# First output units of an attention and spectral-mixing kernel: another order of products, copies and PSUM banks

## The chip, the cores and the metric

The kernel runs on one core of a Trainium2 chip. The metric is the device time of one execution in microseconds (us). Before the change three runs gave 438.65, 438.73 and 439.03 us, median 438.73 us. Engines are called as in the profile: PE (TensorE, matmuls), DVE (VectorE), ACT (ScalarE), POOL (GpSimd), SP (SyncE). POOL and SP also issue DMAs; SP issues all DMAs that write the output.

## The reference

Sliding-window attention with a linear distance bias is followed by a mixing of the 64 lowest Fourier modes along the sequence, and by a channel product with ReLU. Batch 8, 8 heads of 64 channels, so 512 channels; 576 positions; float32 in and out.

```
scores = where(0 <= i-j < 128, q k^T / sqrt(D) - slope_h |i-j|, -1e9)
x      = softmax(scores) v                     # [8, 576, 512], heads side by side
X      = rfft(x, axis=positions)
Y[:64] = X[:64] (w_r + i w_i)                  # one 512x512 pair of matrices per mode
u      = x + irfft(Y)
out    = u + relu(u @ w_ch)
```

The weights w_r and w_i are 64 matrices of 512x512 each, 134 MB in all; the output is 9.44 MB.

## The kernel before, in words

**Two long stages and a tail.** The attention runs while the first weights load. Then the products of the modes with their weights (L886) follow the weight DMAs, sixteen groups of four modes ("quads"). What the tail needs is prepared beside them: `project` leaves `XW` = x @ w_ch and `augment` changes `x` in place, both with the lower 32 modes already in. The upper 32 modes come late. Their spectra stand as rows of `Z` (per batch pair), and `ZW` holds Z @ w_ch. The last quad, modes 60 to 63, depends on the last weight matrix; its rows are `yq`, and `yw` is yq @ w_ch.

**The tail: 18 output units.** A unit is two batches by 128 positions by 512 channels, 512 KB of output. Units 8 and 17 hold the last 64 positions of four batches each. Units 0 to 3 need batches 0 and 1, units 4 to 7 batches 2 and 3, unit 8 batches 0 to 3, units 9 to 12 batches 4 and 5, units 13 to 16 batches 6 and 7, unit 17 batches 4 to 7. For each unit:

- `mm` in PSUM is XW, brought in by products with an identity (`begin`, `restore`, L762; L758 for units 8 and 17), plus the late modes from `ZW` (`channels`, L659; L772). `activate` then makes `r` = relu(mm) on ACT (L802).
- `yy` in PSUM is x plus the late modes from `Z` (`add_tokens`, `finish_tokens`, the same lines).
- `finish` adds `o` = yy + r on DVE (L842) and SP writes `o` to the output (L844; L851 for units 8 and 17). `o` has 5 buffers.

`mm` and `yy` are each one tile of two PSUM banks (`pair`), one bank per batch, n = 0 and 1. There are two slots of four banks. Slot 0 is opened within the last quad, slot 1 after the last quad's own products.

**Modes 60 to 63.** Units 0 and 1 get them by one product per half with `FM` (`last_rows`, L786) from `yq` and `yw`. All others read them from `Z` and `ZW`, into which `patch` copies them by small DMAs on SP or POOL (L648), one per batch: 6 KB or 2 KB or 8 KB.

**Unit 0 is done in halves and by other engines.** `with_tokens` adds the last modes to yy of half n and ACT copies it into `o` (L816); `finish_first` adds the last modes to mm of half n, DVE computes o = max(mm, 0) + o (L823), and SP writes that half (L825). Units named in `HALVES` run ACT, DVE and the output DMA once per half instead of once per unit.

**What sets the order.** All engines run their instructions in program order, written out by hand. Before, the order behind the last weight product is: transposes of the last quad (L962); Z patches of batches 0 to 6; yy of unit 0 half 0; yw (L601, L603); mm of unit 1; ZW patches (batches 0 and 1 by SP, 2 to 7 by POOL), Z patch of batch 7; `finish_first`, which between its halves does half 1 of `with_tokens`; then `activate(1)`, `finish(1)`, `activate(2)`, and for j = 3 to 17 `activate(j)`, `finish(j-1)`; at the end `finish(17)`. So mm of unit j stands ahead of yy of unit j-1 on PE. A PSUM slot of mm is free again when ACT has read it, one of yy when DVE has read it.

## Time and profile before

| what | value |
|---|---|
| median of 3 runs | 438.73 us |
| the profiled execution's own time | 437.99 us |
| its span in the profile | 436.1 us |
| busy: PE, DVE, ACT, POOL | 316.2, 184.5, 162.3, 90.2 us |
| last weight product starts (L886) | 402.42 us |
| first output DMA issued (L825) | 406.89 us |
| last output sum on DVE (L842) | 429.48 to 430.16 us |
| output: 23 DMAs, 10 of 256 KB and 13 of 512 KB | 9.44 MB |
| median from issue to landing, 256 KB and 512 KB | 3.4 and 5.0 us |

Positions in time are counted from the start of the span. The profiled execution took 1.9 us more than its span and 0.7 us less than the median of the runs. Durations of single instructions come from this one execution. An idle time that the profile puts down to an engine whose work was long done was a wait for something else that it stood together with, often a DMA.

### The profile page before, as it was taken

How to read it: one execution, taken by the hardware profiler on the slowest of the kernel's cores; microseconds unless marked ns; L12 is line 12 of the kernel's file. 1: busy time of each engine (PE TensorE's matmuls, PEld its weight loads, DVE VectorE, ACT ScalarE, POOL GpSimd, SP SyncE). 2: the span in 40 equal slices, each digit the busy share in tenths (PEclk: the TensorE clock that was granted, in tenths of full speed). 3: DMA queues.
4: the chain of work that ended last, by engine and by line, in shares of the span. 5: the costliest groups of instructions: out<-in, count | busy, mean ns of one | idle time of the engine just before them, and what ended most of it. 6: DMA issues, size and time to landing. Idle time of an engine off the chain costs nothing.

```text
span 436.1 us, 8292 instructions
## 1 busy us (share of the span) xinstructions
PE 316.2 (73%) x3488; PEld 177.7 (41%) x3509; DVE 184.5 (42%) x332; ACT 162.3 (37%) x211; POOL 90.2 (21%) x170
## 2 busy tenths in 40 slices
PE   5589899979686635543442487999889999788982
PEld 4367677757565312111111133444434444334430
DVE  7789799887783301000000021322213233122684
ACT  6949899988681000000000011322222322102780
POOL 8701010103424002222112110101111110012600
PEclk9969999999999955555555569999999999989997
DMA  8999999999999999999999999999999999998598
GB/s 285 326 311 310 290 316 300 307 298 299 252 217 212 215 215 213 214 214 214 215 212 214 214 215 214 215 214 215 215 214 214 215 215 215 213 215 153 190 378 311
DMA packets 50453, 105.54 MB, mean 242 GB/s; under 512 B 4032, under 2 KB 21072, under 8 KB 50416
## 3 DMA queue, kind: packets, MB, share of 16 engines
q0 software_dynamic: 19440, 68.41, 77.9%
q1 hardware_dynamic: 30976, 36.60, 25.3%
q8 instruction: 27, 0.44, 0.4%
q14 instruction: 10, 0.08, 0.1%
HBM read 162.53 MB, written 9.44 MB: 394 GB/s over the span
## 4 chain that ended last, share of the span: by engine, by line
DMA 71%; PE 10%; DVE 8%; issue 5%; POOL 2%; ACT 1%; SPq 1%; DVEq 0%; POOLq 0%; ACTq 0%
DMA w<-in_moe_w_i_dram 42%; DMA wch<-in_moe_w_ch_dram 8%; DMA qr<-in_q_dram 7%; DMA vr<-in_v_dram 6%; DVE o L842 3%; DMA qr<-in_moe_w_i_dram 3%; PE my L702 2%; DMA vr<-in_moe_w_r_dram 2%; DMA kr<-in_k_dram 2%; DVE vb L246 1%; PE acc L886 1%; PE av L344 1%; POOL Z L648 1%; PE my L659 1%; DVE att L318 1%
## 5 line engine op out<-in xcount | busy, mean ns | idle before, releaser
L886 PE MATMUL acc<-w,XC 128*32 128x512 bf16 x456 | 80.3, 478 | 68.5 <-DMA w<-in_moe_w_i_dram 34.2
L886 PEld LDWEIGHTS <-XC 128*32 128x32 bf16 x508 | 38.4, 147 | 109.2 <-issue 82.8
L307 ACT ACTIVATE att<-sc 128x1024 bf16<-128x1024 f32 x64 | 64.1, 1032 | 9.7 <-PE sc L297 9.6
L636 ACT CAST ZW<-zw 128x512 bf16<-128x512 f32 x8 | 4.7, 585 | 142.9 <-PE zw L634 142.9
L344 PE MATMUL av<-vb,att 128*128 128x132 bf16 (+1 forms) x576 | 38.4, 217 | 13.3 <-DVE x L360 8.6
L344 PEld LDWEIGHTS <-att 128*128 128x128 bf16 x704 | 36.6, 98 | 18.7 <-DVE x L360 12.0
L608 DVE TENSOR_SCALAR yq<-acc 128x512 bf16<-128x512 f32 x14 | 9.6, 687 | 81.8 <-PE acc L886 81.8
L702 PE MATMUL my<-wch,xT 128*64 128x512 bf16 x288 | 34.5, 381 | 5.7 <-ACT x L733 4.2
L711 ACT CAST XW<-my 128x512 bf16<-128x512 f32 x36 | 19.3, 589 | 50.5 <-PE my L659 50.5
L683 DVE COPY xT<-tr 128x1024 bf16<-128x1024 bf16 x18 | 12.4, 692 | 54.9 <-PE tr L681 54.9
L269 ACT COPY qkT<-tp 128x1152 bf16<-128x1152 bf16 x30 | 33.5, 1116 | 4.1 <-PE tp L263 3.6
L491 POOL DMA_DIRECT2D w<-in_moe_w_r_dram x22 | 15.6, 710 | 72.1 <-PE acc L886 46.1
L491 POOL DMA_DIRECT2D w<-in_moe_w_i_dram x23 | 16.3, 709 | 64.1 <-PE acc L886 45.3
L297 PE MATMUL sc<-qkT 64*64 64x256 bf16 (+2 forms) x640 | 25.1, 263 | 4.8 <-ACT qkT L269 1.2
L360 DVE TENSOR_TENSOR x<-av,rec 128x640 bf16<-128x640 f32 x32 | 26.4, 825 | 1.1
L702 PEld LDWEIGHTS <-xT 128*64 128x64 bf16 x288 | 17.1, 109 | 21.5 <-issue 9.1
L246 DVE CAST vb<-vr 64x1024 bf16<-64x1024 f32 x32 | 22.6, 708 | 0.2
L733 ACT CAST x<-my 128x512 bf16<-128x512 f32 x18 | 10.5, 585 | 31.6 <-PE my L659 31.6
L297 PEld LDWEIGHTS <-qkT 64*64 64x64 bf16 x640 | 14.5, 109 | 19.1 <-issue 16.0
L734 DVE CAST x<-my 128x512 bf16<-128x512 f32 x18 | 12.4, 692 | 21.7 <-PE my L659 21.7
L842 DVE TENSOR_TENSOR o<-yy,r 128x1024 f32<-128x1024 f32 (+1 forms) x20 | 20.3, 1059 | 2.1 <-ACT r L802 1.9
L318 DVE TENSOR_TENSOR att<-att,mask 128x1024 bf16<-128x1024 bf16 x32 | 20.5, 682 | 0.0
(137 smaller groups left out, 424.7 us busy)
## 6 DMA issues: line engine op xcount, KB each, us to landing
w<-in_moe_w_i_dram POOLq DMA_DIRECT2D x23, 1024.0 KB, 36.2
w<-in_moe_w_r_dram POOLq DMA_DIRECT2D x22, 1024.0 KB, 35.6
qr<-in_q_dram SPq DMA_DIRECT2D x16, 576.0 KB, 7.9
kr<-in_k_dram SPq DMA_DIRECT2D x16, 576.0 KB, 7.9
w<-in_moe_w_r_dram POOLq DMA_DIRECT2D x16, 512.0 KB, 14.2
vr<-in_v_dram SPq DMA_DIRECT2D x56, 128.0 KB, 7.6
w<-in_moe_w_i_dram POOLq DMA_DIRECT2D x13, 512.0 KB, 24.0
out_dram<-o SPq DMA_DIRECT2D x13, 512.0 KB, 5.0
```

The costliest lines, as they stand in the source:

```text
L246: nc.vector.tensor_copy(self.vb[u % 2][row, :, :, :, W * half : W * half + D], src[row, :2])
L269: (self.nc.vector.tensor_copy if u < 2 and w == "q" else self.nc.scalar.copy)(dst.rearrange("q h (p j) -> q h p j", j=TPP), tp.rearrange(" ...
L297: nc.tensor.matmul(sc[64 * half : 64 * half + 64, e, j * 256 + c0 : j * 256 + c0 + n], lhsT=qkT[row, 1, h, k0 + j : k0 + P : 2], rhs=qkT[r ...
L307: self.nc.scalar.activation(self.att[u % 2][:, kt * 8 * P : (kt + 1) * 8 * P], sc.rearrange("p e n -> p (e n)"), AF.Exp, scale=1.0 / math. ...
L318: nc.vector.tensor_tensor(out=rows, in0=rows, in1=self.table[:, heads], op=ALU.mult)
L344: nc.tensor.matmul(bank[:, qt * W : qt * W + rhs[j].shape[1]], lhsT=att[:, o : o + P], rhs=rhs[j], start=(n == 0 and j == 0), stop=(n == l ...
L360: nc.vector.tensor_tensor(out=self.x[:, b, :, cs].rearrange("p t (h d) -> p h t d", h=2), in0=tiles[:, :, :, :D], in1=rec.unsqueeze(-1).br ...
L491: nc.gpsimd.dma_start(out=t.rearrange("p s a e -> p s (a e)"), in_=w[kinds.pop()][m : m + 2].rearrange("m (p a) e -> p m (a e)", a=4))
L702: nc.tensor.matmul(mm[ROWS[half]], lhsT=lhsT, rhs=wch[:, dt], start=(dt == 0), stop=False, skip_group_check=True,)
L711: nc.scalar.copy(XW[:, j, n], mms[n])
L842: nc.vector.tensor_tensor(out=o[:, c], in0=yy[:, c], in1=r[:, c], op=ALU.add)
L886: nc.tensor.matmul(into[32 * (m % 4) : 32 * (m % 4) + 32], lhsT=XC[:, c0 : c0 + 31 * NM + 1 : NM], rhs=wq[t][a], start=(ri == 0 and a == 0 ...
```

## The change

- Each slot is opened by `open_slot` with separate tiles for the two halves ("joint" false: four one-bank tiles mm0, mm1, yy0, yy1), used by unit 0 and unit 1. Later the slot is closed and opened again with pair tiles as before (slot 0 behind `finish_first`, slot 1 behind `finish(1)`).
- Half 1 of unit 0's `with_tokens` moves ahead of unit 1's mm (and out of `finish_first`), and its copy goes to DVE; half 0's stays on ACT.
- Unit 1's `last_rows` and relu alternate by halves.
- `finish` is split: `sums(j)` has yy's products. Order on PE: yy(1), yy(2), mm(2), then for j = 3 to 17 mm(j), yy(j). On DVE and ACT the units' order is as it was.
- Unit 3 joins `HALVES`: two relus, two sums and two output DMAs of 256 KB.
- Patches: SP has only ZW of batch 0. POOL issues Z 1, Z 2, ZW 1, Z 3, ZW 2, ZW 3, then Z 4, Z 5, ZW 4, ZW 5, Z 6, Z 7, ZW 6, ZW 7.

```diff
-        HALVES = (1, 2, len(units) - 1)
+        HALVES = (1, 2, 3, len(units) - 1)
         def pair(tag, slot=0):
-            return heads[tag][slot].tile([P, 2, DM], FP32, tag=tag, name=tag)
+            pool, joint = slots[slot]
+            if joint:
+                t = pool.tile([P, 2, DM], FP32, tag=tag, name=tag)
+                return t, t[:, 0], t[:, 1]
+            return (None, *(pool.tile([P, DM], FP32, tag=tag + str(n), name=tag)
+                            for n in range(2)))
+        def open_slot(slot, joint, **kw):
+            if slot in slots:
+                opened[slot].close()
+            opened[slot] = mctx.enter_context(ExitStack())
+            slots[slot] = opened[slot].enter_context(tc.tile_pool(
+                name=f"s{slot}{joint:d}", bufs=1, space=PSUM, reuse_waits="tile", **kw)), joint
+        def hold(j):
+            slot = idle.pop(0)
+            mms[j] = pair("mm", slot), slot
         def begin(j):
-            slot = idle.pop(0)
-            mm = pair("mm", slot)
-            mms[j] = mm, slot
-            restore(mm, j, XW[:, j])
+            if j not in mms:
+                hold(j)
+            restore(mms[j][0], j, XW[:, j])
         def activate(j):
-            if j == 1:
-                last_rows(mms[j][0], j, heads["yw"])
-            else:
+            if j != 1:
                 begin(j)
                 channels(j)
...
             for c in parts(j):
-                nc.scalar.activation(r[:, c], mm[:, c], AF.Relu)
+                if j == 1:
+                    last_rows(mm, 1, heads["yw"], (c.start,))
+                nc.scalar.activation(whole(r, c), part(mm, c), AF.Relu)
-        def with_tokens(o, n):
+        def with_tokens(o, n, copy):
             last_rows(yys[0][0], 0, heads["yq"], (n,))
-            nc.scalar.copy(o[:, n], yys[0][0][:, n])
+            copy(o[:, n], yys[0][0][1 + n])
         def finish_first(o):
...
                 nc.sync.dma_start(out=out[n, :P], in_=o[:, n])
-                if n == 0:
-                    with_tokens(o, 1)
-        def finish(j):
-            b, st = units[j]
+        def sums(j):
             if j not in yys:
                 take(j)
             add_tokens(j)
             finish_tokens(j)
+        def finish(j):
+            b, st = units[j]
...
-        patch([(nc.gpsimd, b) for b in (2, 3, 4, 5, 6)], yq, lambda b: Z[:, b // 2, 1], 6)
+        patch([(nc.gpsimd, 2)], yq, lambda b: Z[:, b // 2, 1], 6)
...
-        with_tokens(first, 0)
+        with_tokens(first, 0, nc.scalar.copy)
         for i, c in enumerate(sides):
             zl = zps.tile([P, DM], FP32, tag=f"z{i}", name=f"zl{i}")
             late_channels(zl, yT, yw, c)
+        with_tokens(first, 1, nc.vector.tensor_copy)
...
         channel_rows = partial(patch, rows=yw, dst=lambda b: ZW[:, b // 2, 1])
-        channel_rows([(nc.sync, 0), (nc.sync, 1)] + [(nc.gpsimd, b) for b in range(2, B)])
-        patch([(nc.gpsimd, 7)], yq, lambda b: Z[:, b // 2, 1], 6)
+        channel_rows([(nc.sync, 0), (nc.gpsimd, 1)])
+        patch([(nc.gpsimd, 3)], yq, lambda b: Z[:, b // 2, 1], 6)
+        channel_rows([(nc.gpsimd, b) for b in (2, 3)])
+        for b in range(4, B, 2):
+            patch([(nc.gpsimd, b), (nc.gpsimd, b + 1)], yq, lambda b: Z[:, b // 2, 1], 6)
+            channel_rows([(nc.gpsimd, b), (nc.gpsimd, b + 1)])
         finish_first(first)
+        open_slot(0, True)
+        hold(2)
         activate(1)
+        sums(1)
+        sums(2)
         finish(1)
+        open_slot(1, True, side="right")
         activate(2)
+        finish(2)
+        take(3)
+        hold(3)
         for j in range(3, len(units)):
             activate(j)
-            finish(j - 1)
-        finish(len(units) - 1)
+            sums(j)
+            finish(j)
```

More of the change, by code (lines that the diff above doesn't have):

```diff
@@ L581 @@
         ps = pctx.enter_context(tc.tile_pool(name="fps", bufs=1, space=PSUM))
-        heads, free, idle = {}, [], []
+        heads, slots, opened, free, idle = {}, {}, {}, [], []
         def late_end(acc):
@@ L734, in augment, with part, whole @@
             nc.vector.tensor_copy(src[:, 1], ys[1])
-        HALVES = (1, 2, len(units) - 1)
+        HALVES = (1, 2, 3, len(units) - 1)
         mms, yys, rs = {}, {}, {}
         def pair(tag, slot=0):
-            return heads[tag][slot].tile([P, 2, DM], FP32, tag=tag, name=tag)
+            pool, joint = slots[slot]
[10 more added lines that the diff above has]
+                name=f"s{slot}{joint:d}", bufs=1, space=PSUM, reuse_waits="tile", **kw)), joint
+        def part(t, c):
+            return t[0] if c.stop - c.start == 2 else t[1 + c.start]
+        def whole(t, c):
+            return t if c.stop - c.start == 2 else t[:, c.start]
         def take(j):
@@ L757, in restore @@
                 if units[j][1] == FULL:
-                    nc.tensor.matmul(dst[:, n], lhsT=pairs, rhs=src[:, n],
+                    nc.tensor.matmul(dst[1 + n], lhsT=pairs, rhs=src[:, n],
                                      start=True, stop=False, skip_group_check=True)
@@ L762, in restore @@
                     nc.tensor.matmul(
-                        dst[ROWS[row], n], lhsT=ident[ROWS[n], ROWS[n]],
+                        dst[1 + n][ROWS[row]], lhsT=ident[ROWS[n], ROWS[n]],
                         rhs=src[ROWS[n], row], start=True, stop=False, skip_group_check=True,
@@ L771, in late_modes @@
                 if st == FULL:
-                    nc.tensor.matmul(dst[:, n], lhsT=FC, rhs=rows[:, b // 2 + n, 1],
+                    nc.tensor.matmul(dst[1 + n], lhsT=FC, rhs=rows[:, b // 2 + n, 1],
                                      start=False, stop=True, skip_group_check=True)
@@ L775, in late_modes @@
                 for row in range(2):
-                    spread(dst[:, n], row, b + n, 1, st, row, rows)
+                    spread(dst[1 + n], row, b + n, 1, st, row, rows)
         def channels(j):
@@ L785, in last_rows @@
             for n in sides:
-                nc.tensor.matmul(ps[:, n], lhsT=FM[:, n, st * P : (st + 1) * P], rhs=rows,
+                nc.tensor.matmul(ps[1 + n], lhsT=FM[:, n, st * P : (st + 1) * P], rhs=rows,
                                  start=False, stop=True, skip_group_check=True)
@@ L811, in finish_tokens @@
             late_modes(yys[j][0], j, Z)
-        def with_tokens(o, n):
+        def with_tokens(o, n, copy):
             last_rows(yys[0][0], 0, heads["yq"], (n,))
-            nc.scalar.copy(o[:, n], yys[0][0][:, n])
+            copy(o[:, n], yys[0][0][1 + n])
         def finish_first(o):
-            (mm, mm_slot), (_, yy_slot) = mms.pop(0), yys[0]
+            (mm, mm_slot), (_, yy_slot) = mms.pop(0), yys.pop(0)
             for n in range(2):
                 last_rows(mm, 0, heads["yw"], (n,))
-                nc.vector.scalar_tensor_tensor(out=o[:, n], in0=mm[:, n], scalar=0.0,
+                nc.vector.scalar_tensor_tensor(out=o[:, n], in0=mm[1 + n], scalar=0.0,
                                                in1=o[:, n], op0=ALU.max, op1=ALU.add)
                 nc.sync.dma_start(out=out[n, :P], in_=o[:, n])
-                if n == 0:
-                    with_tokens(o, 1)
-            del yys[0]
             idle.append(mm_slot)
             free.append(yy_slot)
-        def finish(j):
-            b, st = units[j]
+        def sums(j):
             if j not in yys:
@@ L841, in finish @@
             for c in parts(j):
-                nc.vector.tensor_tensor(out=o[:, c], in0=yy[:, c], in1=r[:, c], op=ALU.add)
+                nc.vector.tensor_tensor(out=whole(o, c), in0=part(yy, c), in1=whole(r, c),
+                                        op=ALU.add)
                 if st < FULL:
@@ L869 @@
                     pctx.close()
-                    head = mctx.enter_context(
-                        tc.tile_pool(name="hps", bufs=1, space=PSUM, reuse_waits="tile"))
-                    heads.update(mm=[head], yy=[head])
+                    open_slot(0, False)
                     idle.append(0)
@@ L974 @@
             late_channels(zl, yT, yw, c)
+        with_tokens(first, 1, nc.vector.tensor_copy)
         zctx.close()
         lctx.close()
-        last = mctx.enter_context(
-            tc.tile_pool(name="tps", bufs=1, side="right", space=PSUM, reuse_waits="tile"))
-        heads["mm"].append(last)
-        heads["yy"].append(last)
+        open_slot(1, False, side="right")
         idle.append(1)
```

## The prediction

> **What bounds the kernel now.** The page first: its second part shows DMA at 8 or 9 tenths in nearly all slices, with one hole in the third slice from the end. The last weights set when that hole begins (the last L886 product starts at 402.42), and the change touches nothing ahead of it. So I cut the end of the span into windows. Columns: us, busy time of PE, PEld, DVE, ACT, POOL with instruction counts, granted clock, DMA share, GB/s.

> ```profile
> 402.50:407.50 5.00, 3.86 (x31) 1.79 (x35) 1.45 (x4) 2.47 (x7) 3.69 (x8) 1.00 0.05 10
> 407.50:408.80 1.30, 1.17 (x20) 0.53 (x20) 1.00 (x3) 1.30 (x3) 1.30 (x3) 1.00 0.63 214
> 408.80:412.00 3.20, 3.20 (x56) 1.61 (x49) 2.82 (x5) 3.20 (x5) 1.74 (x4) 1.00 0.86 293
> 412.00:416.00 4.00, 3.80 (x48) 1.46 (x45) 3.95 (x5) 3.30 (x4) 0.00 (x0) 1.00 1.00 369
> ...
> 428.00:434.00 6.00, 0.63 (x3) 0.10 (x1) 2.11 (x3) 0.00 (x0) 0.00 (x0) 0.81 1.02 379
> 434.00:436.10 2.10, 0.00 (x0) 0.00 (x0) 0.00 (x0) 0.00 (x0) 0.00 (x0) 0.50 0.06 23
> ```

> The reader is to see three stretches: five us almost without DMA while PE, ACT and DVE make the first results; 4.5 us in which the output flows at 214 and 293 GB/s; and from 412 on a flow of about 379 GB/s to the end. The last sum on DVE ends at 430.16, the flow near 434: behind DVE there are 4 us of queued output. A shorter DVE or ACT step after 413 therefore buys nothing. The time is: start of the output flow, plus 9.44 MB at 379 GB/s (24.9 us), plus what the flow lacks near its start. The lack: from the first bytes at 407.7 to 412.0 the two windows moved 0.28 and 0.94 MB where 4.3 us would carry 1.63, so 0.41 MB or 1.08 us; from 412 to 416 another 0.1. Some 1.2 us are to be had, and more only by starting earlier.

> The chain of waits names DVE L842 for the largest part of the tail; the timeline corrects it. By engine:

> ```profile
> 406.64 0.81 PE L786 MATMUL mm<-F,FM 128*128 128x512 bf16 x3 [0.57 <-DVE o L823]
> ```
> ```profile
> 405.90 0.69 DVE L823 SCALAR_TENSOR_TENSOR o<-mm,o 128x512 f32<-128x512 f32 x1 [1.83 <-DMA Z<-yq]
> 407.13 0.69 DVE L823 SCALAR_TENSOR_TENSOR o<-mm,o 128x512 f32<-128x512 f32 x1 [0.54 <-PE mm L786]
> 408.12 1.29 DVE L842 TENSOR_TENSOR o<-yy,r 128x512 f32<-128x512 f32 x2 [0.30 <-ACT r L802]
> 409.79 7.09 DVE L842 TENSOR_TENSOR o<-yy,r 128x512 f32<-128x512 f32 x7 [0.38 <-ACT r L802]
> ```
> ```profile
> 406.11 0.58 ACT L816 COPY o<-yy 128x512 f32<-128x512 f32 x1 [0.72 <-PE yy L786]
> 407.49 6.90 ACT L802 ACTIVATE r<-mm 128x512 f32<-128x512 f32 x9 [0.79 <-PE mm L786]
> ```
> ```profile
> 405.61 1.22 SPq L648 DMA_DIRECT2D ZW<-F  x2
> 406.89 1.32 SPq L825 DMA_DIRECT2D out_dram<-o  x2
> 408.84 8.44 SPq L844 DMA_DIRECT2D out_dram<-o  x9
> ```

> PE's product for half 1 of unit 0 waited 0.57 us until DVE had read half 0: another bank, but the same tile. Behind it on PE queue the two products of unit 1, so ACT's relu and DVE's sums start late. DVE idles between its first sums (0.54, 0.30, 0.38), and each idle becomes a hole in the output flow. The 1.05 us that DVE idles before 423.84 is put down to ACT's r, which was ready two units earlier; it waits for one of the five o buffers, so for the output DMA.

> **The change part by part.** All starts that follow are estimates from rows of this execution.

> (1) yy half 1 moved ahead of unit 1's mm. The eight L601 products start 0.11 apart from 403.95, so PE is free at 404.82. One 128x512 product costs 0.23 (L786 at 405.47, the next at 405.70) and a change of stationary shape 0.09 (404.91 against 404.82). Unit 1's mm starts 0.23 later, at 405.14, its late modes at 405.38, and unit 0's mm half 0 at about 405.70 instead of 405.47. Cost 0.23 on the path to the first sum: it is done at 406.1 instead of 405.86.

> (2) The copy of half 1 goes from ACT (0.58) to DVE. The row nearest is L823, same source and size: 0.69. It runs from 405.3 to 406.0, under step 1's product, so nothing; without that cover it would cost up to 0.69 ahead of the first output. ACT loses the copy at 406.11.

> (3) First output. The sum runs 406.12 to 406.81 (before 405.90 to 406.59). Before, SP issued it only at 406.89, since its second ZW patch held it until 406.83; that patch goes to POOL. New issue about 406.85. Steps 1 and 3 cancel: the flow starts where it did, give or take 0.2.

> (4) Separate tiles. The wait of 0.57 goes. Half 1's product runs at 405.92, and its sum is next late on DVE alone: back-to-back half sums start 0.61 apart (408.12, 408.73), so 406.73 instead of 407.13. Gain 0.40.

> (5) Unit 1. Its last rows run at 406.14 and 406.36, relu from 406.55 (before 407.49), yy from 406.67 to 407.3. DVE is again what is late: sums at 407.34 and 407.95 instead of 408.12 and 408.73. Gain 0.78.

> (6) Unit 2. yy(2), 0.43 for its eight products, now stands ahead of mm(2); mm(2) must wait for slot 0 in any case, until DVE ends unit 0 at 407.42. mm(2) from 407.5, its ZW products at 407.75, relu at 408.2, sums at 408.8 and 409.4 instead of 409.79 and 410.40. Gain 1.0, if the ZW row of batch 1 is there by 407.75. POOL issues it when unit 1's mm has read ZW, near 405.85, behind Z 1 and Z 2 (done at 404.9), instead of SP at 406.27. From issue to landing, the 8 KB Z patch on POOL took 1.7 in the quiet stretch; POOL's ZW patches took 2.1 to 3.4 within the output flow. The output begins at 407.7, so it is nearest to the 1.7, with 2.1 to 2.4 possible. I take 2.0, landing 407.85: cost 0.1. Ends: 0, and with 3.4 (landing 409.25) 1.5 at this step.

> [...]

> (7) Unit 3 by halves. On DVE 2 x 0.61 for 1.13 (the spacing of full sums, 410.99 to 412.12), on ACT 2 x 0.49 for 0.90; the first half leaves 0.5 us sooner. Sums at 410.0 and 410.6, then unit 4 at 411.2 instead of 412.12: gain 0.9. The two more instructions on DVE and SP lie beside the flow.

> (8) mm(j) then yy(j) instead of a unit's lead. o(j) frees yy of j+2; behind it PE does yy(j+2) and mm(j+3), ACT the relu. Before, with the same pair of products, DVE ended at 422.79 and the relu that followed ended at 424.97: 2.2 us. Two full sums on DVE cover 2 x 1.13, two units of output 2 x 1.38. So nothing; at units 8 and 9, whose products cost 0.43 more, DVE comes late by 0.3 to 0.5, and I find 0.4 us of queued output left there. If that cover were gone it would cost at most 0.1 to 0.3.

> (9) POOL's order. ZW 2 and 3 are issued at about 406.85 and 407.4 as before. Z 4 to ZW 7 end near 412, within the flow instead of before it; with 3.4 to land they are there by 415.5, and unit 9 reads them at 416, units 13 and on after 421. Nothing.

> Sum as output flow: 256 KB take 0.69 us at 379 GB/s. Bytes move 0.85 to 0.9 us after issue (406.89 against 407.7). Issues at 406.85, 407.45, 408.05, 408.65, 409.5, 410.1, 410.75, 411.35 let eight pieces follow one another without a hole from 407.7 to about 413.25; unit 4's issue at 412.45 is due at 413.35. Lack 0.1 there, 0.1 for ZW 1 and about 0.05 for the fact that each single DMA in flight alone ran at 360 rather than 379, instead of 1.2. Gain 0.95: 437.99 becomes 437.04 in terms of the profiled execution. That execution lies 0.74 below the median, so in terms of runs 437.8.

> **The rivals.**

> *The wait stays in another form* (437.4 to 438.3 in runs). If product and sum of unit 0's halves are still held together, or the reopened slot waits for DVE's last read where I let it wait for the copy, PE's rest begins at 406.9: relu(1) at 407.5 as before, but ACT and SP are relieved and yy(2) is ready, unit 4's sum at 411.8 instead of 412.12. Gain 0.35 to 0.6, time 438.25. For it: mm(1) at 404.91 shows waits tile by tile at an earlier reopening, which speaks against; that half 1 waited at all shows that the waits are wider than the data, which speaks for.

> *ZW of batch 1 lands late* (slower). Place: PE at mm(2), with everything behind it. By step 6, landing at X puts unit 4's output issue at X + 4.75 and its bytes at X + 5.65. Before, they were served at 414.5. Break even is X = 408.85, 3.0 us after issue; at the 3.4 of the slowest ZW patch the loss is 0.4 (439.1, within the 0.2%), and from 4.0 it is slower by over 0.2%: 439.7. For it: patches got slower from 2.1 to 3.4 as the output flow set in, and POOL queues a wait for PE ahead. Against: it is issued two us before the first output byte. [...]

> *The lost lead shows* (438.4). If step 8's loop were 3.0 instead of 2.2, DVE would fall to the flow's pace of 1.38 per unit; beyond that the flow would have holes all along. The row is far from it.

> **How the numbers follow.** 0.2% is 0.88 us, about what a measurement of this kernel can tell from no change. Forecast, gain 0.9 to 1.4: chance 0.50. The wait in another form, and the lost lead, together 0.28: within 0.2%. ZW late but under 4 us: 0.12, within 0.2%. ZW later: 0.10, slower. The likeliest time is 437.8, with its own range 437.3 to 437.9; it lies close to the bound, which the sum passes by less than 0.1 us, so faster and same are near each other. Low end 437.2: all of 1.2, and the flow's start 0.3 earlier if SP and step 1 are both kinder. High end 439.2 takes in the late patch at 3.4.

> **What would show it.** Right: no idle on PE before L786 for DVE; DVE without idle from about 405.3 to 411; first output issue at 406.8 to 406.9; unit 4's sum near 411.2; the window from 408.8 to 412 near 370 GB/s; flow over by 433. Wrong: PE idle at mm(2) for a DMA, first output after 407.1, a dip in GB/s near 417 to 420, or DVE idle for ACT in the steady part.

## The result, and the profile after

The changed kernel takes 441.58 us (median of 14 runs, 439.33 to 443.47) against 438.69 us before (14 runs, 438.14 to 440.11): ratio 1.0057, 95% interval 1.0041 to 1.0073. The change makes the kernel slower, by about 2.5 us by this ratio; the medians lie 2.9 us apart. Its runs also scatter over 4 us, those of before over 2.

The profiled execution took 442.13 us, its span 440.3. The last weight product starts 0.58 us later than in the profile of before (403.00 against 402.42), ahead of anything that was changed. From there to the end of the span it is 37.3 us against 33.7. I count times as "+x us" behind the start of the last weight product where kernels are compared. The same stretches of the tail, moved by 0.5 to 0.6 us; columns as above:

```profile
403.00:408.00 5.00, 4.74 (x44) 2.14 (x44) 2.37 (x6) 2.75 (x7) 2.20 (x5) 1.00 0.04 8
408.00:409.40 1.40, 1.40 (x28) 0.67 (x24) 1.25 (x2) 0.51 (x2) 1.40 (x4) 1.00 0.82 287
409.40:412.60 3.20, 1.21 (x16) 0.38 (x14) 2.48 (x4) 1.78 (x4) 3.20 (x7) 1.00 0.87 292
412.60:416.60 4.00, 3.14 (x38) 1.94 (x41) 1.64 (x2) 2.05 (x2) 0.85 (x2) 0.72 0.59 212
416.60:420.60 4.00, 4.00 (x41) 2.35 (x37) 3.16 (x3) 3.07 (x3) 0.00 (x0) 0.85 0.89 329
420.60:424.60 4.00, 3.46 (x60) 1.74 (x56) 3.75 (x4) 3.11 (x5) 0.00 (x0) 1.00 0.88 322
424.60:428.60 4.00, 3.41 (x56) 1.76 (x55) 3.75 (x4) 3.63 (x4) 0.00 (x0) 1.00 0.79 288
428.60:434.60 6.00, 3.16 (x32) 1.09 (x20) 4.57 (x5) 2.43 (x4) 0.00 (x0) 1.00 1.04 381
```

The reader is to see that the flow starts better than before (287 GB/s where it was 214), then PE has 1.21 us of work in 3.2, and from 412.6 the flow falls to 212 GB/s, where before it had reached 369. The next three rows miss another 50, 51 and 92 GB/s against the 379, 373 and 380 of before:

```profile
416.00:420.00 4.00, 3.93 (x56) 1.93 (x59) 3.84 (x4) 3.50 (x5) 0.00 (x0) 1.00 1.03 379
420.00:424.00 4.00, 3.68 (x60) 1.73 (x52) 2.95 (x4) 3.57 (x5) 0.00 (x0) 1.00 1.02 373
424.00:428.00 4.00, 2.49 (x21) 0.88 (x22) 3.92 (x4) 2.06 (x3) 0.00 (x0) 1.00 1.03 380
```

The hole from 412.6 is 0.63 MB and the three rows behind it are 0.77 MB, or 1.7 and 2.0 us at 380 GB/s. The second and third rows together are ahead of before by only 0.12 MB (0.3 us).

The timeline of PE around the hole, that of POOL, and that of DVE, in the changed kernel:

```profile
409.54 0.40 PE L659 MATMUL yy<-Z,FT 64*64 64x512 bf16 x3
410.25 0.41 PE L784 MATMUL mm<-XW,ident 64*64 64x512 bf16 x4 [0.31 <-ACT r L824]
410.52 0.40 PE L659 MATMUL mm<-ZW,FT 64*64 64x512 bf16 x2
413.46 0.40 PE L659 MATMUL mm<-ZW,FT 64*64 64x512 bf16 x2 [2.54 <-DMA ZW<-F]
```
```profile
404.40 1.07 POOL L648 DMA_DIRECT2D Z<-yq  x2 [1.33 <-ACT yq L981]
406.93 0.59 POOL L648 DMA_DIRECT2D ZW<-F  x1 [1.47 <-ACT F L603]
407.51 0.51 POOL L648 DMA_DIRECT2D Z<-yq  x1
408.01 1.13 POOL L648 DMA_DIRECT2D ZW<-F  x2
```
```profile
405.82 0.69 DVE L838 COPY o<-yy 128x512 f32<-128x512 f32 x1 [1.17 <-PE yy L808]
406.70 1.29 DVE L845 SCALAR_TENSOR_TENSOR o<-mm,o 128x512 f32<-128x512 f32 x2 [0.19 <-PE mm L808]
407.96 1.29 DVE L864 TENSOR_TENSOR o<-yy,r 128x512 f32<-128x512 f32 x2
409.74 2.48 DVE L864 TENSOR_TENSOR o<-yy,r 128x512 f32<-128x512 f32 x4 [0.49 <-ACT r L824]
414.96 2.36 DVE L864 TENSOR_TENSOR o<-yy,r 128x1024 f32<-128x1024 f32 x2 [2.73 <-PE mm L659]
```

Unit 4's mm does two of its four products at 410.52, those of batch 2. The other two need the ZW row of batch 3 and come at 413.46. POOL's third ZW patch, batch 3, is the second of the pair at 408.01, so it goes out at 408.60. The trace's landing records have 15 of its 16 parts by 411.26 and the last at 413.42. Before, the same patch went out at 407.42, as the second of the six in the row below, and all 16 parts were there by 409.55.

```profile
406.85 3.17 POOL L648 DMA_DIRECT2D ZW<-F  x6
```

The tile's view gives issue to landing as minimum, median and maximum, first before, then after:

```profile
DMA to landing us min/median/max: 2.1/2.8/3.4
```
```profile
DMA to landing us min/median/max: 1.7/3.7/4.8
```

A DMA of POOL, and one of SP to the output, has 16 parts with a landing record each, as many as the core has DMA engines. That each engine carries one part is my assumption, and no record shows it, since none names the engine of a part; such an engine is called a "ring" here. What goes with the late sixteenth part is in the records of the instruction queue (q8): one packet of 16 KB at 410.25 that took 1.47 us. Before there is one too, at 409.72 with 1.19 us; the ZW rows that units 4 to 7 need had landed by then. DMAs issued around the packet have one part late in both kernels: before, the ZW row of batch 5 had 15 parts by 410.71 and the last at 411.85; after, the last part lay 1.9 to 2.2 us behind the fifteenth for all DMAs issued from 408.6 to 409.7. Such packets come about every 256 PE instructions, weight loads counted (in the trace of before 188 to 316 apart, 256 on the mean), so I read them as fetches of PE's instructions. PE lost nothing by the one at 409.72: before, it worked all through it (3.20 us of 3.20 from 408.8 to 412). Of the DMAs issued around it, the last part came up to 1.1 us behind the fifteenth, and around the one at 410.25 in the changed kernel up to 2.2 us. That packet and late part share a ring is read from the times alone, and the experiments below move the one and look for the other.

PE's clock comes on top. PE stood from 410.9 to 413.46, and the granted clock then was half for 3.41 us from 414.38: the shares 0.72 and 0.85 in the fourth and fifth rows above, and L659 products of 631 ns where the median is 376. A second profile of the changed kernel (below) had a wait of 2.15 us and no half clock. In the traces of before and after the clock's steps lie multiples of 3.41 us apart. Of the stretches of 3.41 us on that grid that ran at full clock, half clock followed each of the 12 in which PE stood for 1.88 us or more, one of two with 1.8, and none with 1.70 or less. The one that ended at 414.38 began at 410.97 and held 2.49 us of PE's wait; in the second profile a boundary at 411.11 cuts the wait into 0.95 and 1.21 us. That fits, but it does not prove that the wait's place on the grid decided.

### The profile page after: what moved, and what is told of

It is laid out like the page before. It is cut to its first block, busy times and chain, and to the rows that moved or that the text cites. A ratio compares the mean times of both kernels' runs of the same rounds, so it can differ in the third digit from the quotient of the medians.

```text
span 440.3 us, 8317 instructions
## 1 busy us (share of the span) xinstructions
PE 321.5 (73%) x3509; PEld 180.1 (41%) x3509; DVE 185.9 (42%) x334; ACT 162.1 (37%) x211; POOL 92.6 (21%) x171
## 3 DMA queue, kind: packets, MB, share of 16 engines
HBM read 162.53 MB, written 9.44 MB: 391 GB/s over the span
## 4 chain that ended last, share of the span: by engine, by line
DMA 67%; PE 13%; DVE 9%; issue 5%; ACT 2%; POOL 1%; SPq 1%; DVEq 0%; POOLq 0%; ACTq 0%
DMA w<-in_moe_w_i_dram 42%; DMA qr<-in_q_dram 9%; DMA wch<-in_moe_w_ch_dram 8%; DMA vr<-in_v_dram 3%; DMA vr<-in_moe_w_r_dram 2%; PE av L344 2%; PE my L702 2%; DVE vb L246 2%; DVE att L318 2%; PE acc L907 1%; DVE x L360 1%; DMA out_dram<-o 1%; DMA ZW<-F 1%; PE my L659 1%; DVE o L864 1%
## 5 line engine op out<-in xcount | busy, mean ns | idle before, releaser
L344 PEld LDWEIGHTS <-att 128*128 128x128 bf16 x704 | 37.3, 99 | 16.3 <-DVE x L360 10.7
L269 ACT COPY qkT<-tp 128x1152 bf16<-128x1152 bf16 x30 | 33.5, 1115 | 3.0 <-PE tp L263 2.4
L297 PE MATMUL sc<-qkT 64*64 64x256 bf16 (+2 forms) x640 | 25.5, 267 | 2.5 <-ACT qkT L269 1.6
L284 PE MATMUL sc<-bias,ident 128*128 128x512 bf16 x64 | 20.1, 398 | 1.3 <-ACT att L307 1.3
```

The costliest lines, as they stand in the source:

```text
L269: (self.nc.vector.tensor_copy if u < 2 and w == "q" else self.nc.scalar.copy)(dst.rearrange("q h (p j) -> q h p j", j=TPP), tp.rearrange(" ...
L284: nc.tensor.matmul(sc[:, e], lhsT=self.ident, rhs=self.bias[:, hv].rearrange("p j n -> p (j n)"), start=True, stop=False, skip_group_check ...
L297: nc.tensor.matmul(sc[64 * half : 64 * half + 64, e, j * 256 + c0 : j * 256 + c0 + n], lhsT=qkT[row, 1, h, k0 + j : k0 + P : 2], rhs=qkT[r ...
L344: nc.tensor.matmul(bank[:, qt * W : qt * W + rhs[j].shape[1]], lhsT=att[:, o : o + P], rhs=rhs[j], start=(n == 0 and j == 0), stop=(n == l ...
```

## The experiments

Ratios are against runs of the kernel before on the same chip, and are not those of the two medians given; brackets are 95% intervals. Theory A: unit 4 waits for the ZW row of batch 3, which the new patch order sends later, into the time of PE's instruction fetch. Rival B: the new order of products costs. Rival C: patches are late under the output flow, fetch or not.

**1. The changed kernel with the old patches.**

```diff
-        patch([(nc.gpsimd, 2)], yq, lambda b: Z[:, b // 2, 1], 6)
+        patch([(nc.gpsimd, b) for b in (2, 3, 4, 5, 6)], yq, lambda b: Z[:, b // 2, 1], 6)
...
-        channel_rows([(nc.sync, 0), (nc.gpsimd, 1)])
-        patch([(nc.gpsimd, 3)], yq, lambda b: Z[:, b // 2, 1], 6)
-        channel_rows([(nc.gpsimd, b) for b in (2, 3)])
-        for b in range(4, B, 2):
...
+        channel_rows([(nc.sync, 0), (nc.sync, 1)] + [(nc.gpsimd, b) for b in range(2, B)])
+        patch([(nc.gpsimd, 7)], yq, lambda b: Z[:, b // 2, 1], 6)
```

> The changed kernel with only the patches put back: SP issues ZW 0 and 1, POOL issues Z 1 to 6, then ZW 2 to 7, then Z 7. Theory A (the loss is unit 4 waiting on PE for the ZW row of batch 3: in the changed kernel POOL issues it at 408.60 instead of 407.42, and one of the 16 DMA rings, which fetches 16 KB of instructions from 410.25 on, lands its part at 413.42, while the other 15 land by 411.26): ZW 3 is out 1.2 us sooner, lands before the fetch, PE does not wait; the gain of the prediction appears, 437.8 us, ratio to before 0.998. Rival B (the new order of products, mm(j) and yy(j) without a unit's lead, is what costs): still near 441.5, ratio 1.006.

Measured 438.78 against 438.43, ratio 1.0009 [0.9991, 1.0027]. The loss is gone, so it hung on the patches and not on the order of products: B falls. But the gain does not appear either. DVE no longer idles at unit 4 (its eight sums from 409.74 run on to 416.8):

```profile
407.79 1.29 DVE L864 TENSOR_TENSOR o<-yy,r 128x512 f32<-128x512 f32 x2
409.74 7.06 DVE L864 TENSOR_TENSOR o<-yy,r 128x512 f32<-128x512 f32 x8 [0.66 <-ACT r L824]
```

In this profile the tail is 33.73 us against 33.67 before. The last part of the last output landed at +32.39 against +32.75, so 0.36 sooner. Then SP's closing waits took 0.5 us: they ask the DMA semaphores in a fixed order, and the one more output DMA had put the last one on the semaphore that is asked first, with eight waits of 0.06 us behind it.

**2. The kernel before with the new patches.** The opposite edit.

> The kernel before with only the new order of the patches. Theory A: ZW 3 goes out about 0.9 to 1.2 us later than before, near 408.4, so it is in flight when the instruction fetch takes one ring near 409.7: PE waits at unit 4's mm by 1 to 3 us and the time is 439.5 to 442. Rival B: as before, 438.7.

Measured 439.44 against 438.43, ratio 1.0021 [1.0004, 1.0039]: the patch order alone costs 1.0 us, less than half of the loss. In its one profile ZW 3 had landed at +7.67, in time for unit 4; what grew there is the lag of the sixteenth part around the fetch, up to 2.1 us behind the fifteenth instead of up to 1.1, and the tail was 34.50. That the lag is what costs the 1.0 us is not shown. So the late row at unit 4 needs both edits, but not because it is asked for sooner: unit 4's first ZW product runs at +7.48 before and in this run, and at +7.51 in the changed kernel. With the new products ZW 1 and, behind it, ZW 3 go out 0.21 us later (+5.59 instead of +5.38), since step 1's product stands ahead of unit 1's mm, and that is enough to be caught by the fetch.

**3. and 4. The fetch moved.** 56 small products with an unused result under the weight DMAs, 112 PE instructions, in the changed kernel and in the one before.

```diff
                 k = 8 * g + i
+                if g == 10:
+                    for _ in range(7):
+                        wt = ps.tile([P, DM], FP32, tag="my", bufs=2, name="my")
+                        nc.tensor.matmul(wt[:, :32], lhsT=ident, rhs=ident[:, :32],
+                                         start=True, stop=True)
```

> The changed kernel with 56 more small products (32 columns, result unused) within the eleventh group of four modes, under the weight DMAs: 112 more PE instructions, so that every later fetch of PE's instructions comes 112 instructions sooner, and the one at 410.25 falls near 405, where DMA is all but idle. Patches as in the changed kernel. Theory A with the fetch as the cause: ZW 3 lands at about 411.1 on all rings, unit 4 waits 0.6 us instead of 2.9, PE's clock is not halved at 414; 438.0 to 438.6 us. Rival C (patches of POOL are late under the output flow with or without a fetch): 440 us or more. Rival B: 441.5.

> The kernel before with the same 56 small products, as control. Theory A: nothing waits for the stalled ring there before unit 4 but the output flow itself, so 438.2 to 438.8 us; it also shows what the 56 products cost by themselves, expected nothing. Rivals B and C: 438.7.

Measured 439.11 (ratio 1.0013 [0.9998, 1.0028]) for the changed kernel and 439.07 (1.0014 [1.0002, 1.0027]) for the control. The control is 0.6 us slower, where I had expected nothing; whether the products cost it or the fetches that they moved is not told apart. Beside this control nothing of the changed kernel's loss is left. The fetch came at -1.3 us instead of +7.3, further off than meant, and the next at +12.2, within the output flow; there, and no longer around +7, the sixteenth parts are late (1.92 us for the output DMA issued at +11.09). With the patches exactly as changed, PE now waits 0.41 us for the row of batch 3 instead of 2.54:

```profile
410.36 0.40 PE L659 MATMUL mm<-ZW,FT 64*64 64x512 bf16 x2
411.17 0.40 PE L659 MATMUL mm<-ZW,FT 64*64 64x512 bf16 x2 [0.41 <-DMA ZW<-F]
```

The patch, issued at +5.59 as in the changed kernel, had all 16 parts at +8.30 (2.71 us) instead of +10.42. So the fetch is what makes the late row expensive; C holds for the 0.41 alone.

**5. The rows regrouped.** Z 3 goes out with Z 2, and ZW 1, 2, 3 follow one another on POOL.

```diff
-        patch([(nc.gpsimd, 2)], yq, lambda b: Z[:, b // 2, 1], 6)
+        patch([(nc.gpsimd, 2), (nc.gpsimd, 3)], yq, lambda b: Z[:, b // 2, 1], 6)
...
-        channel_rows([(nc.sync, 0), (nc.gpsimd, 1)])
-        patch([(nc.gpsimd, 3)], yq, lambda b: Z[:, b // 2, 1], 6)
-        channel_rows([(nc.gpsimd, b) for b in (2, 3)])
+        channel_rows([(nc.sync, 0)] + [(nc.gpsimd, b) for b in (1, 2, 3)])
```

> The changed kernel with one regrouping of POOL's patches: Z 3 goes out with Z 2 ahead of yw, then ZW 1, ZW 2, ZW 3 follow each other, the rest as changed. ZW 3 is issued 0.5 us sooner than in the changed kernel (about 5.1 us behind the last weight product instead of 5.6) and would land on 15 rings near 7.3, just when the instruction fetch starts. Theory A: between the changed kernel and the one with the old patches: unit 4 waits 0 to 2 us, 438.5 to 440 us with a wide scatter, since it hangs on the fetch by tenths. Rival E (POOL's later patches, Z 4 to ZW 7, make the loss by their share of the rings): as the changed kernel, 441.

Measured 438.53 against 438.67, ratio 1.0002 [0.9986, 1.0019]. One small patch in another place in POOL's queue, half a microsecond, takes away the whole loss (the changed kernel on the same chip, next run, was at 440.76). The expected wide scatter of 438.5 to 440 us was too gloomy: ZW 3 goes out at +5.05 and is complete at +7.64, although the fetch starts at +6.99; the next patch, issued at +5.59, has its last part 1.36 us behind the fifteenth. So not every DMA in flight is hit: a patch that is issued early enough gets through. Rival E (the later patches) falls as the cause of the loss, since they stayed late.

**7. The changed kernel once more.**

> The changed kernel itself, beside the others on one chip. Theory A: 441 to 442 us, in its profile unit 4's mm waits for the ZW row of batch 3, and PE's clock falls to half behind that wait if it lasts over 2 us.

Measured 440.76 against 438.67, ratio 1.0044 [1.0029, 1.0058]. Its profile shows the same wait, 2.15 us, but no half clock in the rows behind it, which I had expected for waits over 2 us:

```profile
412.32 0.40 PE L659 MATMUL mm<-ZW,FT 64*64 64x512 bf16 x2 [2.15 <-DMA ZW<-F]
```
```profile
411.90:415.90 4.00, 2.95 (x50) 1.63 (x50) 2.08 (x2) 2.86 (x3) 0.83 (x2) 1.00 0.56 203
415.90:419.90 4.00, 3.87 (x46) 1.56 (x40) 3.56 (x4) 2.65 (x3) 0.00 (x0) 1.00 1.00 371
```

The flow is back at 371 GB/s in the row where the first profile had 329, and the tail is 35.4 us instead of 37.3. Of these 2 us, 0.4 were there at unit 4's sum (+11.54 against +11.96), and at +21, behind the stretch of the half clock, the first profile's flow was 0.9 us late (4.58 MB moved against 4.93). The last 1.0 us came from +21 to +23 at full clock: SP's issue of the output DMA at +20.32 took 1.76 us, where the like one in the second profile (+20.45) took 0.68, and the flow nearly stopped until it was done. A fetch began at +20.37 there; what held SP is not shown. Two profiles cannot say how often the half clock or the slow issue comes, but together they are enough for the scatter of the runs.

**6. and 8. Looking for the gain.** The regrouped kernel with 40 small products (the fetch then at +3.0); the old patches with unit 3 in one piece, which takes away the extra output DMA and with it the 0.5 us of closing waits.

> The same with 40 small unused products under the weights (80 PE instructions), which bring the fetch to about 1 to 4 us behind the last weight product, where DMA is idle. Theory A: unit 4's wait is gone, its sum starts at 9.2 or sooner behind the last weight product (9.7 before); time 437.8 to 438.5. Theory D (the end is set by the one ring that carries PE's fetches, so holes in the mean flow behind the first fetch are no loss to recover): the end behind the last weight product is not more than 0.4 us sooner than the 33.7 of before unless the second fetch also moves; its lag at the end decides.

> The changed kernel with the old patches and with unit 3 in one piece again. In the run with the old patches the last output DMA lay on the DMA semaphore that SP's closing waits ask for first, so that eight more waits of 0.06 us came behind the last landing (0.5 us); one output DMA less puts it last in that row again. Theory D: the end behind the last landing 0.5 us shorter, 33.2 us behind the last weight product instead of 33.7, and 438.3 instead of 438.8 in time. Rival: unit 3's halves fill a hole in the flow, and without them the flow ends 0.3 us later, so that nothing is won.

Measured 438.33 (ratio 0.9991 [0.9978, 1.0004]) and 438.80 (0.9997 [0.9981, 1.0012]). Neither is shown to be faster than before. In the profile of 6 the late part has moved with the fetch into the quiet stretch: the Z patch issued at +1.96 has 15 parts at +3.50 and the last at +5.36. In the profile of 8 the closing waits behind the last landing are gone, and the tail is 33.59 us; the expected 33.2 did not come, since the end lies 1.13 us behind the last landing (0.91 before).

**9. to 12. What sets the end.** Theory D: the one ring that carries PE's fetches sets the end; the last part of the last output landed 0.8 us behind the median part before and 1.0 after. Theory F: the five o buffers, which hand such a lag on to the other rings. Run 9 adds seven small products ahead of mm in each of the units 9 to 17 of the kernel before; 10, 11 and 12 have eight buffers for o in the regrouped kernel, in the kernel before, and in the regrouped kernel with the 40 products.

```diff
             mms[j] = mm, slot
+            for _ in range(7 if j >= 9 else 0):
+                nc.tensor.matmul(mm[:, 0, :32], lhsT=ident, rhs=ident[:, :32],
+                                 start=True, stop=True, skip_group_check=True)
```
```diff
-            o = heads["out"].tile([P, 2, DM], FP32, tag="o", bufs=5, name="o")
+            o = heads["out"].tile([P, 2, DM], FP32, tag="o", bufs=8, name="o")
```

The line that makes unit 0's o is changed in the same way.

> The kernel before with seven small products (32 columns, overwritten by the unit's own first product) ahead of mm in each of the units 9 to 17: 126 more PE instructions in the last 17 us, where PE has time, so that a third fetch of 16 KB falls near 25 us behind the last weight product. Output flow, DVE and ACT are not touched. Theory D (the end is set by the one DMA ring that carries PE's fetches): that ring's lag at the last output grows from 0.8 to 1.3 to 2 us, and the end moves from 33.7 to 34.2 to 34.8 behind the last weight product; 439.2 us. Rival (the end is the mean flow): as before, 438.7.

> The regrouped changed kernel (Z 3 early, ZW 1 to 3 in a row) with eight buffers for o instead of five. In its five-buffer run DVE idled 0.7 us before unit 13, until the slow ring had landed unit 8, and the flow fell to 353 GB/s from 17.6 to 21.6 us behind the last weight product. Theory F (the five buffers hand the slow ring's lag on to the other 15): no dip, flow at 380 there, 0.2 to 0.4 us sooner, 438.2. Theory D: the dip goes, but the slow ring ends as late as before, 33.4 us behind the last weight product, time unchanged.

> The kernel before with eight buffers for o. DVE's idle of 1.05 us before unit 13 goes under both theories. Theory F: 0.2 to 0.4 us sooner than 438.6. Theory D: unchanged.

> All that helped together: the regrouped changed kernel, the fetch brought to 3 us behind the last weight product by 40 small products, eight buffers for o. Theory F: 437.9 us, ratio to before 0.998. Theory D: 438.3, ratio 0.999, as with five buffers.

Measured, against 438.95: 439.16 (ratio 0.9996 [0.9982, 1.0011]), 438.85 (1.0000 [0.9981, 1.0018]), 438.81 (0.9995 [0.9975, 1.0016]), 439.15 (1.0000 [0.9975, 1.0025]). F is not borne out: with eight buffers DVE runs through in the kernel before, without the 1.05 us of idle time that is seen in the profile with five, and nothing is seen to be won.

```profile
410.10 18.87 DVE L842 TENSOR_TENSOR o<-yy,r 128x512 f32<-128x512 f32 x18 [0.39 <-PE yy L659]
```

The profiles' tails are no shorter with eight buffers (33.53 us against 33.45 in the regrouped kernel, 34.03 against 33.67 before, 34.45 against 33.60 with the 40 products). The timed runs cannot tell: the 0.2 to 0.4 us that F expects are a ratio of 0.9991 to 0.9995, inside the intervals of 10 and 11, and its 0.998 for 12 is inside that of 12.

D stays open. The profiles speak for it: in 9 a third fetch at +25.5 goes with a last part that lands 1.4 us behind the median part of its DMA (0.8 before) and a tail of 34.74 us; in 12 a fetch at +29.2 leaves the median part of the last DMA at +31.4, 0.5 us sooner than before, and the last part at +33.5, 0.8 us later. The timed runs of 9 don't follow: an extra 1.07 us would be 1.0024, outside its interval.

## Why the prediction was wrong, by its own steps

**Steps 1 to 5 held.** Unit 0's first sum and its first output DMA were foreseen at +3.7 and +4.43 and came at +3.70 and +4.42. The wait of 0.57 us on PE is gone; the row of DVE from 406.70 on shows the first four half sums running on. Unit 1's sums were foreseen at +4.92 and +5.53 and came at +4.96 and +5.57.

**Step 6 was right in kind and too small.** Unit 2's sums came at +6.74 instead of +6.38. POOL started the DMA 0.5 us behind the wait at the head of its queue: unit 1's mm had read ZW at +3.4, ZW 1 went out at +3.93. It took 1.70 us to land, less than the 2.0 I took. The cost was 0.4 us, not 0.1. From issue to landing SP's ZW patch in this trace took 1.75 us, so no more for POOL; from the end of the wait to landing it was 1.78 us for SP (+3.38 to +5.16) and 2.20 for POOL (+3.43 to +5.63).

**Step 7 held**, with unit 3's sums at +7.94 and +8.54, 0.36 later as step 6 makes it. **Step 8 held** too: in experiment 5 unit 8 comes 0.43 us late on DVE, and the flow is at 385 GB/s.

**Step 9 is the one that failed.** "ZW 2 and 3 are issued at about 406.85 and 407.4 as before", it says, and its price is "Nothing". They went out at +5.01 and +5.59 instead of +4.44 and +5.01, because ZW 1, waiting for PE, and Z 3 stood ahead of them. Nearly all of that is the 0.5 us that POOL took from the end of its wait to the issue of ZW 1, which no step has. The landing of ZW 3 was not set against unit 4's product at all. And I priced landings by the rows 2.1 to 3.4 without asking what made the 3.4: the two patches with 3.4 were issued at +6.05 and +6.57, just ahead of the fetch at +7.30, and their last parts came 1.14 and 0.87 us behind the fifteenth. A half microsecond in the queue became 2.5 us on PE, and unit 4's sum came at +11.96 instead of +8.8.

**The rival with a late ZW row** named the right mechanism at the wrong batch: batch 1 at unit 2 instead of batch 3 at unit 4. Its condition was a landing of 4.0 us or more behind issue, which it had for rare; the row of batch 3 took 4.8 and 4.4 us in the two profiles.

**The gain of 0.95 us did not come even without the late row.** In experiment 5 unit 4's output DMA goes out at +10.43; before it was +10.95, and foreseen was +10.03. The 0.4 is step 6's. By +13.6 us its flow has moved 2.89 MB against 2.69 before, 0.5 us at 380 GB/s; at the last landing 0.2 us are left, and in time it is 1.0002 [0.9986, 1.0019]. Where the rest goes is not settled. The prediction took the mean flow for the bound, though the last part was 0.2 to 1.4 us behind the fifteenth at every landing on record after 411 in the trace that it was made from.

## What to carry to other kernels

When transfers are reordered, price each by when its reader needs it and by what else is in flight at that moment (here one packet of 16 KB, with the last of 16 parts up to 2.2 us late); a transfer that waits for another engine should not stand ahead of one that waits for nothing and is needed soon. A landing time with a long tail (2.1/2.8/3.4) is a question, not a range: look up which instances are slow, and whether a change moves new ones into that time. And in a stretch that is bound by DMA, ask for the slowest of the 16 parts of each DMA too, not only for the mean GB/s.
